# A new order and new engines for every command of a hand-scheduled attention and maxout kernel, later casting loads, no zero products, and a hint for the last jump

## The chip, the core and the metric

The kernel runs on one core of a Trainium2 chip. The metric is device time in microseconds (us): the median of several runs. The core has TensorE (PE in the profile, with its weight loads as PEld), VectorE (DVE), ScalarE (ACT), GpSimd (POOL) and SyncE (SP). A "q" behind a name (SPq, POOLq, ACTq) means that the engine issues a DMA or handles an instruction that its sequencer does alone.

## The reference

`q`, `k` and `v` have 4 batches, 8 heads, 768 positions and 64 numbers per head, in float32. Half the meaning lies in `is_retrieval`: heads 0, 2 and 6 are retrieval heads with a full causal mask, the other five are streaming heads, where a position sees the 4 first positions and the 64 latest ones.

```python
scores = scale * np.matmul(q, k.transpose(0, 1, 3, 2))
causal = rel >= 0
stream_keep = causal & (is_sink | in_win)      # n_sink = 4, window = 64
scores = np.where(mask[None], scores, -1000000000.0)
a = np.exp(scores - max); a = a / (sum(a) + 1e-09)
x = matmul(a, v)                               # to (3072, 512), heads side by side
h = np.maximum(np.maximum(x @ w1, x @ w2), x @ w3)   # 512 -> 768, three times
out = h @ w_out                                # 768 -> 512, float32
```

## The kernel before

The kernel is compiled for the pattern of retrieval heads that it expects (`GUESS`). It computes everything with that pattern, then compares the flags that it was given and checks that all sums of exponentials are in a sane range. Only if one of the two fails does a general, slow block run behind a jump at the end (L780); with these inputs it does not.

Work is done by batch `b`, and in each batch by halves of 384 positions. For each half, attention comes first, and then the products with the four weight matrices, here called the FFN of that half: 18 groups of four products (L387; matrix 0, 1 or 2 times one block of 128 hidden columns), each followed by a copy or a maximum out of PSUM (L395, L397), and 3 output blocks of 128 rows (L412), each copied out (L418) and stored (L419). That makes 21 steps for each of 8 halves, 168 in all. In batch 0 the 18 groups go through matrix 0 first, then 1, then 2.

There is no scheduler. A long list of strings, `PROGRAM`, gives the order in which commands are recorded, and with it the order of each engine's queue: every engine takes its own instructions strictly in that order. A letter at the end of a command picks the engine: `d` VectorE, `a` ScalarE, `p` GpSimd. The commands are:

- `hl half pair n ss`: plain loads of k and q of batch 0, by SyncE (L185). `cast` makes them float16 (L199), `turnp` transposes them on TensorE and copies the result out (L217, L220), `kx0` builds the extra keys (sinks and previous window, L476, L481).
- `s0 half unit pairs`: one unit of scores of batch 0, products on TensorE (L511, L526) and exponentials on ScalarE (L546). `k0` multiplies a mask in (L558).
- `load b quad`: k and q of a later batch, cast on the way by GpSimd's DMA queue (L236). `turn` transposes them on VectorE (L251), `kx` builds extra keys (L488, L493), `s` is a unit of scores (L597, L614), `k` a mask (L627).
- `load_v` loads v by SyncE (L274), `v` and `y` cast it into the two operands that the second product takes (L436, L448, L450).
- `av b half pair`: the product of weights and v (L646), reciprocal and scaling (L651, L653), and with `D` a transpose by SyncE's DMA queue (L659); without it, `x` transposes on TensorE (L669, L672).
- `w i`: a casting load of weight matrix i by GpSimd's queue (L361; `w 3` is the output matrix, L356).
- `f e`: the next step of the FFN; `e` is the engine of its copy.
- `idle n`: n products of a tile of zeros, 128x512, whose result nothing reads (L295).
- `clear`, `cleark`, `strip`: constant fills on VectorE. `flags`: the comparison of the flags. `check`, `verdict`: the check of the sums. `gs`, `gp`: tiny copies that make SyncE or GpSimd wait for a load.

So where a command stands decides both when its own work can begin and what queues behind it. SyncE's DMA issues also wait for an earlier DMA: eight semaphores go round, and a DMA waits for the one eight before it. The staging tiles of the first loads (`pairs2`, two buffers) make `hl 1 2 2` wait for the casts of the pairs loaded by `hl 0 2 2`.

At the end all five engines load the number of mismatches into a register (L779), compare (L780) and, as that number is 0, go to an empty block and jump over the general one to the end.

Of the kernel before, what the change touches and what calls it, by code (L numbers as in the profile page):

```python
# [10 lines left out]
FP32 = mybir.dt.float32  # L11
INT32 = mybir.dt.int32
# [122 lines left out]
def fast(ctx, tc, keep, q, k, v, is_retrieval, n_sink, window, moe_w1, moe_w2, moe_w3, moe_w_out, w_t, woutt, out):  # L135
    nc = tc.nc
    B, H, S, D = q.shape
    DMdl = out.shape[1]
    DF = moe_w1.shape[1]
    P = 128  # L140
# [151 lines left out]
    def idle_work(n):  # L292
        sink = sps.tile([P, 2, 512], FP32, tag="st", name="st")
        for _ in range(n):
            nc.tensor.matmul(sink[:, 0, :], zero[:, 0:P], zero, start=True, stop=True)  # L295
# [650 lines left out]
```

## Time and profile before

| what | value |
|---|---|
| runs | 202.43, 203.18, 203.58 us; median 203.18 |
| the profiled execution | 202.28 us, of which the span from the first to the last instruction is 200.2 |
| PE busy | 180.6 us, 90% of the span |
| DVE, ACT, POOL busy | 152.4, 99.4, 72.3 us |
| first product with weight matrix 0 | 32.23 us into the span |
| last instruction that computes | ends 193.78 us into the span |

The profiled execution is the one whose rows are read below; it is 0.9 us under the median. PE's busy time is an upper bound of its use, since matmuls overlap and their ends are modelled. The program falls into three stretches: a start in which batch 0 is loaded, turned and scored, up to 32 us; a long middle in which TensorE goes from one FFN step to the next with scores and `av` between them; and a tail of some 7 us behind the last product.

### The profile page before, as it was taken

The numbers are of one execution on the slowest core, as the hardware profiler recorded it, in microseconds if no ns is written. First come the engines' busy times: TensorE is split into PE (matmuls) and PEld (weight loads), VectorE is DVE, ScalarE is ACT, GpSimd is POOL, SyncE is SP. The second block draws the span as 40 slices with busy tenths as digits, with TensorE's granted clock in tenths as the row PEclk, the third lists the DMA queues.
The fourth block names the chain that finished last, engine by engine and source line by source line (L and its number), as shares of the span: only waits on it lengthen the run. The fifth ranks groups of instructions, "written<-read, shape, count | busy, mean of one in ns | idle before, by whom it ended". The sixth has DMA issues, their size and how long they took to land.

```text
span 200.2 us, 4763 instructions
## 1 busy us (share of the span) xinstructions
PE 180.6 (90%) x1833; PEld 106.2 (53%) x1833; DVE 152.4 (76%) x357; ACT 99.4 (50%) x170; POOL 72.3 (36%) x111
## 2 busy tenths in 40 slices
PE   0297798999999999999999999999999999999960
PEld 0244365565555644567556645574566467655530
DVE  4897569999797899998479999793667469877800
ACT  2359758723867666174765584537556350000030
POOL 6134724446798215077092049013571030000000
PEclk9999559999999999999999999999999999999996
DMA  5999999999498958996498141014201511340040
GB/s 143 321 166 210 255 203 202 211 142 208 71 212 201 184 102 182 291 230 128 143 233 159 20 144 57 0 24 123 96 0 23 151 65 22 62 157 4 0 160 11
DMA packets 48424, 26.63 MB, mean 133 GB/s; under 512 B 37259, under 2 KB 43915, under 8 KB 48395
## 3 DMA queue, kind: packets, MB, share of 16 engines
q1 hardware_dynamic: 43786, 18.06, 37.0%
q0 software_dynamic: 4192, 7.87, 22.3%
q8 instruction: 16, 0.26, 0.6%
q10 hardware_dynamic: 416, 0.33, 0.5%
q14 instruction: 14, 0.11, 0.2%
HBM read 25.17 MB, written 6.29 MB: 157 GB/s over the span
## 4 chain that ended last, share of the span: by engine, by line
PE 71%; DVE 11%; DMA 8%; issue 3%; ACT 3%; SPq 2%; DVEq 0%; ACTq 0%
PE yy L387 39%; PE yy L412 11%; PE oacc L646 6%; PE st L597 6%; DMA qs<-in_q_dram 6%; PE yst L387 3%; DVE x L653 2%; DMA xT<-x 2%; DVE hT L397 2%; DVE KQ L251 2%; SPq L185 2%; PE st L526 1%; PE tr L217 1%; DVE acc L397 1%; PE yst L412 1%
## 5 line engine op out<-in xcount | busy, mean ns | idle before, releaser
L614 ACT ACTIVATE pt<-st 128x1024 f16<-128x1024 f32 (+2 forms) x51 | 43.5, 907 | 28.0 <-PE st L597 26.4
L627 POOL TENSOR_TENSOR pt<-pt,strip 128x512 f16<-128x512 f16 (+4 forms) x36 | 35.7, 1008 | 55.4 <-ACT pt L614 52.4
L387 PE MATMUL yy<-xT,w2t 128*128 128x384 f16 x180 | 36.0, 326 | 0.4 <-ACT ot L418 0.4
L387 PE MATMUL yy<-xT,w0t 128*128 128x384 f16 x180 | 35.8, 326 | 0.4 <-DMA xT<-x 0.2
L387 PE MATMUL yy<-xT,w1t 128*128 128x384 f16 x180 | 35.2, 326 | 0.2 <-DVE x L653 0.2
L397 DVE TENSOR_TENSOR acc<-yy,acc 128x384 f16<-128x384 f32 x45 | 24.9, 558 | 10.3 <-PE yy L387 4.7
L412 PE MATMUL yy<-woutt,hT 128*128 128x512 f16 (+1 forms) x138 | 31.4, 375 | 0.4 <-DVE hT L397 0.4
L397 DVE TENSOR_TENSOR hT<-yy,acc 128x384 f16<-128x384 f32 x45 | 24.6, 554 | 3.8 <-PE yy L387 1.6
L395 ACT CAST acc<-yy 128x384 f16<-128x384 f32 x26 | 12.4, 486 | 28.1 <-PE yy L387 28.1
L251 DVE STREAM_TRANSPOSE KQ<-kq 128x384 f32<-128x384 f32 x24 | 25.5, 1132 | 0.0
L387 PEld LDWEIGHTS <-w0t 128*128 128x128 f16 x192 | 18.1, 98 | 13.4 <-issue 1.0
L387 PEld LDWEIGHTS <-w1t 128*128 128x128 f16 x192 | 18.1, 98 | 12.9 <-issue 1.1
L387 PEld LDWEIGHTS <-w2t 128*128 128x128 f16 x192 | 17.5, 97 | 12.4 <-issue 1.3
L412 PEld LDWEIGHTS <-hT 128*128 128x128 f16 x150 | 14.0, 98 | 16.1 <-DVE hT L397 1.7
L546 ACT ACTIVATE pt<-st 128x1024 f16<-128x1024 f32 (+4 forms) x28 | 16.2, 636 | 10.1 <-PE st L526 9.8
L646 PEld LDWEIGHTS <-pt 128*128 128x128 f16 x472 | 18.0, 100 | 3.0 <-issue 0.4
L646 PE MATMUL oacc<-va,pt 128*128 128x65 f16 x392 | 19.0, 197 | 0.0
L653 DVE TENSOR_TENSOR x<-oacc,sums 128x384 f16<-128x384 f32 x32 | 17.8, 557 | 1.1
L627 DVE TENSOR_TENSOR pt<-pt,strip 128x256 f16<-128x256 f16 (+4 forms) x33 | 13.9, 437 | 5.6 <-ACT pt L614 5.6
L597 PE MATMUL st<-KQ 32*128 32x128 f16 (+2 forms) x342 | 15.1, 257 | 0.0
L597 PEld LDWEIGHTS <-KQ 32*128 32x128 f16 x342 | 8.8, 92 | 6.8 <-issue 5.6
L646 PE MATMUL oacc<-vx,pt 128*128 128x65 f16 x80 | 12.3, 193 | 0.0
(106 smaller groups left out, 196.3 us busy)
## 6 DMA issues: line engine op xcount, KB each, us to landing
out_dram<-ot SPq DMA_DIRECT2D x23, 256.0 KB, 3.1
vs<-in_v_dram SPq DMA_DIRECT2D x21, 256.0 KB, 7.3
ks<-in_k_dram SPq DMA_DIRECT2D x8, 192.0 KB, 3.2
qs<-in_q_dram SPq DMA_DIRECT2D x7, 192.0 KB, 4.4
kq<-in_k_dram POOLq DMA_DIRECT2D x3, 384.0 KB, 5.3
kq<-in_q_dram POOLq DMA_DIRECT2D x3, 384.0 KB, 7.1
kq<-in_k_dram POOLq DMA_DIRECT2D x3, 288.0 KB, 6.4
kq<-in_q_dram POOLq DMA_DIRECT2D x3, 288.0 KB, 7.4
```

Source lines behind the costliest of these rows:

```text
L185: eng.dma_start(out=st[:, h : h + 2], in_=src[0, 2 * hp + h : 2 * hp + h + 2, half * HALF : (half + 1) * HALF].rearrange("h (p j) d -> p h ...
L251: nc.vector.transpose(out=dst.rearrange("c (p j) -> c j p", j=n)[:, j0:j1], in_=src.rearrange("c (j i) -> c j i", i=R),)
L387: nc.tensor.matmul(yy[:, 0:HALF], w_t[wi][:, ks, ni * P : (ni + 1) * P], xT[b, half, ks].rearrange("p a t -> p (a t)"), start=(ks == 0), s ...
L395: copy_out[0](out=acc[ni], in_=yy[:, 0:HALF])
L397: nc.vector.tensor_tensor(out=acc[ni] if wi == 1 else hT[ni], in0=yy[:, 0:HALF], in1=acc[ni], op=ALU.max)
L412: nc.tensor.matmul(yo[:, 0:n], hT[ns][:, tb * P : (tb + 1) * P], woutt[:, ns, c : c + n], start=(ns == 0), stop=(ns == NNB - 1),)
L546: nc.scalar.activation(out=pts[0, half, hp, u][:, r0:r1, c0:c1], in_=sts[hp][:, r0:r1, c0:c1], func=AF.Exp, scale=sc,)
L597: nc.tensor.matmul(sts["XY"[g // 2]][:, g % 2, c0 : c0 + n * P], KQ[rows, 0, ki * P : (ki + 1) * P] if kind == "p" else kx[b % 2][quad][ro ...
L614: nc.scalar.activation(out=pts[b, s, xy][:, r0:r1, c0:c1], in_=st[:, r0:r1, c0:c1], func=AF.Exp, scale=sc,)
L627: engine.tensor_tensor(out=x, in0=x, in1=m, op=ALU.mult)
L646: nc.tensor.matmul(o[:, i, r, 0 : D + 1], at[b, h, kind, ki, qi], vv[:, 0 : D + 1], start=(n == 0), stop=(n == len(todo) - 1), skip_group_ ...
L653: nc.vector.tensor_tensor(out=x, in0=o[:, :, :, 0:D], in1=rc.unsqueeze(3).to_broadcast([P, HB, 2, D]), op=ALU.mult,)
```

## The change

All commands are put into a new order and many get another engine. The parts that can be named:

- The start: the constant fills of the masks (`strip`) come first; the first three loads of v now stand between `hl 0 2 2` and `hl 1 0 2`; `w 0` and `load 1 0`, the first loads that cast, are issued behind the casts of the pair (1, 1), and GpSimd reaches `w 1` and `w 2` behind the casts of the last pair (1, 3). Before, `load 1 0` was issued ahead of `hl 1 2 2`'s q.
- Six units of the second half's scores stand ahead of the first `f`, where eight stood before. All four `av` of the first half still do.
- `idle 2` and `idle 8` are gone.
- Casts of v (`v`): 22 on POOL, 5 on ACT, 5 on DVE; before 10, 11 and 11. Masks (`k`): 33 on POOL and 36 on DVE; before 36 and 33.
- `av 1 1` now stands behind FFN step 47 to 49 (before: 58); `turn 2 1 0 1` directly behind step 19 and close behind `load 2 1` at step 18.
- `flags` moves from the start to the middle. Its result is kept as an integer, and `guess` (behind step 100) loads it on all five engines as a hint for the last jump. `read` (behind step 155, thirteen steps ahead of the end) loads the mismatch count, which before was loaded where the program ends. The general block is now the one that follows the branch, so that the usual way is the branch taken, to the place that was hinted.
- The last half's outputs: block 1 is copied by VectorE, blocks 0 and 2 by ScalarE. Block 2 is still split in two, but now both parts are copied and also stored by ScalarE; before, VectorE copied the second part, and SyncE stored the first.

```diff
 PROGRAM = (
-    "clear 1, flags, hl 0 1 1 ss, clear 0, cast 0 0 pp, turnp 0 0 dd, cleark 0, hl 0 2 2 ss",
-    "strip 0 14, cast 0 2 aa, cast 0 1 ap, turnp 0 1 d, kx0 0 0 a, s0 0 0 0, hl 1 0 2 ss",
-    "cast 1 0 dd, turnp 0 2 ad, turnp 1 0 da, cleark 1, load_v 0 0 0 4, cast 1 1 ap, idle 2",
-    "kx0 0 1 a, s0 0 0 1, cast 0 3 dd, s0 0 1 0, s0 0 1 1, strip 14 28, kx0 1 0 p, load_v 0 0 4 4",
-    "v 0 0 3 d, hl 1 2 2 ss, v 0 0 2 d, turnp 0 3 aa, cast 1 2 dd, load 1 0, s0 1 1 0, s0 0 1 3",
...
-    "turn 1 1 1 1, f d, v 0 1 3 a, idle 8, f d, f a, f a, s 1 1, load_v 1 0, k0 3 1 1 p, av 0 1 3",
...
-    "f d, check, f d, f d, f a, f a, f a, f d, f d, f d, gs 1, verdict, f a, f a, f d, f a, f a",
+    "clear 0, hl 0 1 1 ss, strip 14 28, strip 0 14, cast 0 0 pp, turnp 0 0 aa, cast 0 1 ap",
+    "turnp 0 1 a, hl 0 2 2 ss, cast 0 2 dp, cast 0 3 ad, load_v 0 0 0 4, cleark 0, s0 0 1 1",
+    "kx0 0 0 a, s0 0 0 0, kx0 0 1 p, turnp 0 2 ad, kx0 0 2 p, turnp 0 3 da, hl 1 0 2 ss",
+    "cast 1 0 da, cast 1 1 pp, load_v 0 0 4 4, s0 0 1 2, y 0 0 4:5:1 s d, cleark 1, w 0",
+    "v 0 0 2 a, turnp 1 0 aa, v 0 0 1 p, turnp 1 1 d, s0 0 1 0, load 1 0, kx0 0 3 p, v 0 0 3 p",
+    "hl 1 2 2 ss, cast 1 2 da, s0 0 0 1, y 0 0 5:8:2 r p, y 0 0 4:5:1 r a, clear 1, v 0 0 0 d",
...
+    "check, f d, f d, f d, verdict, f d, f a, f a, f a, f a, f d, read, f d, f d, f a, f a, f a",
+    "f d, f d, f d, f a, f a, f a, f a, f a",
 )
...
-            for c, op, eng in (
-                (0, nc.scalar.copy if last else copy_out[0], nc.sync),
-                (n, nc.vector.tensor_copy, nc.scalar),
-            )[:parts]:
+            for c in range(0, DMdl, n):
...
+                op = copy_out[0] if not last else nc.vector.tensor_copy if tb == 1 else nc.scalar.copy
                 op(out=ot[:, c : c + n], in_=yo[:, 0:n])
-                eng.dma_start(out=out[r0 : r0 + P, c : c + n], in_=ot[:, c : c + n])
+                (nc.sync if parts == 1 else nc.scalar).dma_start(
+                    out=out[r0 : r0 + P, c : c + n], in_=ot[:, c : c + n]
+                )
...
+        nc.vector.tensor_copy(out=flagged, in_=other.to_broadcast([1, 2]))
...
+    def read():
+        found["n"] = nc.values_load(differ[0:1, 0:1], min_val=0, max_val=1 << 20)
+
+    def guess():
+        likely = nc.values_load(flagged[0:1, 0:1], min_val=0, max_val=H)
+        E = mybir.EngineType
+        tc.mark_branch_hint_location("last", likely, [E.SP, E.PE, E.Activation, E.DVE, E.Pool])
...
-        n = nc.values_load(differ[0:1, 0:1], min_val=0, max_val=1 << 20)
-        with tc.If(n > 0, preferred_fallthrough_block=False):
+        with tc.If(n > 0, preferred_fallthrough_block=True, label="last"):
```

More of the change, by code (lines that the diff above doesn't have):

```diff
@@ L292, in idle_work @@
     def idle_work(n):
-        sink = sps.tile([P, 2, 512], FP32, tag="st", name="st")
+        sink = bank([P, 512], FP32, "idl")
         for _ in range(n):
-            nc.tensor.matmul(sink[:, 0, :], zero[:, 0:P], zero, start=True, stop=True)
+            nc.tensor.matmul(sink, zero[:, 0:P], zero, start=True, stop=True)
     warm = consts.tile([P, 2], FP32, name="warm")
@@ L674, in fast @@
     differ = keep.tile([1, 2], INT32, name="differ")
+    flagged = keep.tile([1, 2], INT32, name="flagged")
     found = {}
@@ L744, in fast @@
         w=lambda wi, *p: load_weight(int(wi), *map(int, p)),
+        read=read,
+        guess=guess,
     )
@@ L749, in fast @@
             do[name](*args)
-    return differ
+    return found["n"]
 def kernel(
@@ L774 @@
         xs_dram = tc.dram_tile([B * H, S, D], FP16, name="xs_dram")
-        differ = fast(
+        n = fast(
             tc, keep, q, k, v, is_retrieval, int(n_sink), int(window),
```

90 rows, old and new, of the table PROGRAM are left out of this document.

## The prediction

> **What bounds the kernel now.** I read the page's first part, the busy time by stretch, the chain of waits, and then the groups and DMA issues that the change touches. First the busy time of the engines in six stretches that I cut at the first product with weight matrix 0 (32.23 us) and at the end of the last product (columns: stretch, its length, PE, PEld, DVE, ACT, POOL, granted clock, DMA share, GB/s):
>
> ```profile
> 0.00:4.65 4.65, 0.00 (x0) 0.00 (x1) 2.29 (x10) 1.49 (x2) 3.01 (x13) 1.00 0.50 140
> 4.65:32.23 27.58, 20.91 (x183) 11.73 (x184) 20.93 (x79) 17.75 (x40) 11.94 (x24) 0.81 1.07 228
> 32.23:60.00 27.77, 27.66 (x308) 16.16 (x305) 26.03 (x51) 16.44 (x30) 16.47 (x21) 1.00 0.97 172
> 60.00:100.00 40.00, 39.17 (x444) 22.98 (x443) 33.51 (x70) 24.20 (x38) 16.54 (x22) 1.00 0.83 182
> 100.00:193.36 93.36, 92.85 (x906) 55.27 (x903) 69.20 (x149) 39.47 (x64) 24.30 (x33) 1.00 0.29 75
> 193.36:200.20 6.84, 0.00 (x0) 0.00 (x0) 0.42 (x1) 0.00 (x0) 0.00 (x0) 0.74 0.26 86
> ```
>
> From 32.23 to 193.36 TensorE is busy 27.66 + 39.17 + 92.85 = 159.68 of 161.13 us. So the middle is bound by TensorE, and only 1.45 us of its idle time can be won there. VectorE, with 26.03 of 27.77 us in the third stretch, is the next bound. The start has 4.65 + 6.67 = 11.3 us without a product, and the tail 6.8 us. That is where an order can win; in the middle it can mostly lose. The chain of waits tells what the start waits for:
>
> ```profile
> 3.71 4.42 DMA qs<-in_q_dram
> ...
> 13.65 0.52 ACT kn L199
> ...
> 15.18 6.92 DMA qs<-in_q_dram
> ...
> 22.23 0.55 DVE qn L199
> ...
> 32.68 1.95 PE yy L387 x11
> 34.62 0.43 PE st L526 x7
> ...
> 36.46 0.48 PE st L526 x3
> ...
> 44.86 1.73 PE st L295 x8
> ...
> 193.36 0.42 DVE ot L418
> ```
>
> A late cast (13.65) frees the staging tile for the last pairs of k and q; their q is issued at 15.18 and takes 6.92 us, where an early one takes 4.42. All that follows up to the first product leans on it.
>
> **The start.** SyncE's queue, and then GpSimd's, show what stood ahead of that load and what ran beside it:
>
> ```profile
> 5.81 0.98 SPq L185 DMA_DIRECT2D qs<-in_q_dram  x2
> ...
> 6.87 4.55 SPq L274 DMA_DIRECT2D vs<-in_v_dram  x6
> ```
> ```profile
> 14.07 0.73 POOL L236 DMA_DIRECT2D kq<-in_k_dram  x1 [0.23 <-issue]
> ...
> 20.36 0.82 POOL L361 DMA_DIRECT2D w0t<-in_moe_w_dram  x1
> ...
> 22.46 0.75 POOL L361 DMA_DIRECT2D w1t<-in_moe_w_dram  x1
> 23.20 0.75 POOL L361 DMA_DIRECT2D w2t<-in_moe_w_dram  x1
> ```
> ```profile
> w0t<-in_moe_w_dram POOLq DMA_DIRECT2D x1, 768.0 KB, 9.5
> w1t<-in_moe_w_dram POOLq DMA_DIRECT2D x1, 768.0 KB, 12.0
> w2t<-in_moe_w_dram POOLq DMA_DIRECT2D x1, 768.0 KB, 15.4
> ```
>
> The casting load of 14.07 goes through the same DMA engines (share 1.07). The new order casts the pairs of the first half before everything else, and puts no casting load ahead of the first half's plain loads. So SyncE can issue that q load when the DMA eight places before it has landed. That one is a q load of the pairs before, issued at 5.81 here; with three v loads ahead of it (4.55 / 6 = 0.76 us each) it goes out at 8.1 and, with the early load's 4.42, lands at 12.5. The last q load then lands near 12.5 + 4.4 = 16.9 instead of 22.1: 5.2 us sooner. Not all of it arrives at TensorE. Between 22.2 and 32.2 the chain holds 10 us of casts, copies, exponentials and small products; ScalarE works 17.75 and TensorE 20.91 of the 27.58 us, so they soon become what the start waits for. The bounds are 0 and 5.2 us; I take two thirds, 3.5, as the engines are well filled but 6.67 us without a product lie in the stretch. The first product then stands at 28.7.
>
> The weights cover this. `w 0` waits only for casts that I place at 13 to 14 us, some 6 us sooner than 20.36, so 9.5 us later it lands by 24. `w 1` and `w 2` stand behind the casts of the last pair, at some 20 us: landed by 32 and by 35.4, with 12.0 and 15.4. They are wanted after six and after twelve groups of 0.65 us (1.95 us for eleven products is three groups) with two score units before each, at 28.7 + 4.8 = 33.5 and at 38.3. If the start gained more than 5.0 us, `w 1` would be what is late next.
>
> Two units of scores that stood ahead of the first FFN step now stand behind it, where TensorE is full: 0.43 + 0.48 = 0.9 us back.
>
> `idle 2`, in the start, is counted there. `idle 8` is 1.73 us in a full TensorE, and I take 1.7. Its bounds are 0 and 1.73: if VectorE were late there anyway, the gap stays as a wait.
>
> One rule is weighed here. The rows around the half clock, and at `idle 8`:
>
> ```profile
> 18.00:20.00 2.00, 1.33 (x14) 0.87 (x13) 0.52 (x2) 1.87 (x6) 0.91 (x3) 0.78 1.07 254
> 20.00:24.00 4.00, 3.99 (x31) 1.77 (x29) 1.73 (x4) 3.15 (x8) 3.82 (x7) 0.50 1.21 269
> 24.00:28.00 4.00, 2.93 (x18) 1.39 (x18) 2.96 (x9) 2.10 (x4) 0.00 (x0) 0.50 1.15 202
> 28.00:30.00 2.00, 2.00 (x35) 1.77 (x35) 1.12 (x5) 1.17 (x4) 1.06 (x3) 0.66 1.15 200
> 30.00:32.00 2.00, 1.60 (x26) 1.00 (x28) 1.93 (x6) 1.95 (x4) 2.00 (x5) 1.00 1.16 202
> 44.00:47.00 3.00, 3.00 (x18) 1.57 (x17) 3.00 (x5) 1.82 (x3) 1.50 (x1) 1.00 1.25 190
> ```
>
> The granted clock is 0.50 from 20 to 28 us, though TensorE counts as busy for 3.99 of the first 4 us, and full from 30 us on, with and without zeros. The Trainium skill ("TensorE: Matmul & The Clock Gate", The HAM clock gate) says that about 3.4 us of sustained products release the full clock and that an idle window takes it away; by it, dropping zeros speaks against the change in the gappy start and costs nothing at 44 us. This trace does not bear the first part out: 3.99 busy us released nothing. By the skill's rule a denser start would run at full clock; rival (e) prices that from rows.
>
> **The middle.** The work is the same and only its places change. From the lists: 12 more casts of v and 3 masks fewer on GpSimd, 6 casts fewer each on VectorE and ScalarE, and 3 masks more on VectorE. The prices:
>
> ```profile
> L627 POOL TENSOR_TENSOR pt<-pt,strip 128x512 f16<-128x512 f16 x19 | 22.0, 1163 | 31.2 <-ACT pt L614 31.1
> L436 DVE CAST va<-vs 128x384 f16<-128x384 f32 x11 | 5.7, 524 | 0.0
> L436 POOL CAST va<-vs 128x384 f16<-128x384 f32 x10 | 5.1, 524 | 0.0
> L627 DVE TENSOR_TENSOR pt<-pt,strip 128x512 f16<-128x512 f16 x11 | 5.5, 498 | 2.9 <-ACT pt L614 2.9
> ```
> ```profile
> POOL pt L627 <- ACT pt L614: 52.4, 11, 11.2
> PEld L387 <- issue: 3.3, 12, 0.7
> ```
>
> GpSimd gets 12 x 0.524 - 3 x 1.163 = +2.8 us, VectorE 3 x 0.498 - 6 x 0.524 = -1.7. Both lie beside TensorE's work, with VectorE's share somewhat eased. What can show is a queue: a cast behind a mask whose exponentials come late. The gain is bounded by the 1.45 us of idle time, the loss by one such wait of 11.2 us. An order this dense, started earlier, meets VectorE at its fullest, so I take a loss of 1.0. The two register loads per engine (`guess`, `read`) make TensorE's sequencer stop twice. The nearest row is its waits called issue, up to 0.7 us, so 0 to 1.4; I take 0, as weights loaded ahead cover them, and without that cover they cost the 1.4.
>
> **The tail.** SyncE's waits and the last store:
>
> ```profile
> SPq L780 <- SPq L780: 1.7, 1, 1.7
> ```
> ```profile
> out_dram<-ot ACTq DMA_DIRECT2D x1, 128.0 KB, 3.1
> ```
> ```profile
> 192.75 0.37 ACT L418 COPY ot<-yst 128x256 f32<-128x256 f32 x1
> 193.82 0.37 ACTq L419 DMA_DIRECT2D out_dram<-ot  x1
> ```
>
> The last store lands at 193.82 + 3.1 = 196.9, and the span ends 3.3 us later. SyncE waits 1.7 us at the jump for nobody but itself. The hint can win from 0 to 3.3; I take 1.6, the wait that the row shows, less a little. The Trainium skill ("Runtime: NRT & Kernel Launch", Instruction fetch mechanics) says that a taken branch out of the fetched window stalls for its code. The self-wait agrees; by the skill's rule alone the tail would gain 0. What a hint does to the wait, no row here shows.
>
> ScalarE now copies and stores both parts of the last block: free of the first part at 193.12, it issues to 193.49, copies to 193.86 and issues then, 0.04 behind 193.82. I put 0.1.
>
> **The sum.** -3.5 + 0.9 - 1.7 + 1.0 - 1.6 + 0.1 = -4.8 us against the profiled execution's 202.28 (span 200.2 and 2.08 around it): 197.5. The median shown, 203.18, is 0.9 higher; against it the sum gives 198.4, which is my forecast.
>
> **The rivals.**
>
> (a) The start stays: ScalarE or a TensorE at half clock binds it, whatever lands sooner. For it: 20.91 of 27.58 us busy at a mean clock of 0.81. Against it: the 6.67 us without a product there. Time: 198.4 + 3.5 = 201.9 at most; with half of the gain kept 200.1. I call it 201.
>
> (b) The hint does nothing, and the taken jump waits as before: 198.4 + 1.6 = 200.0.
>
> (c) VectorE takes the start's gain back, being busy 26.03 of 27.77 us already; each us that TensorE comes sooner is then met by a wait on VectorE: 3.5 and 0.9 lost, 202.8. Against it: it loses 1.7 us of casts.
>
> (d) Slower: GpSimd's queue. 22 casts of v stand there among masks that wait for exponentials. In the FFN steps 35 to 47 I count 6 of these casts, 4 masks, 2 k/q issues and more, some 10 us, against some 13 us of TensorE, right ahead of `av 1 1`, which needs all of them. If one wait of 11.2 us falls there, the cover is 3 us, and 8 us show: 206. It decides from 5.8 us on (4.8, and 1.0 for half a percent). Against it: GpSimd is idle for nearly two thirds of the span.
>
> (e) The half clock of 20 to 28 us goes: its 6.92 busy us halve, 3.5 us if TensorE binds there: 194.9.
>
> **How the numbers follow.** The forecast 0.40, (a) 0.18, (b) 0.10, (c) 0.10, (d) 0.16, (e) 0.06. Half a percent, 1.0 us, is about what a measurement of this kernel can tell from no change, so same is 202.2 to 204.2. Faster: 0.40 + 0.18 + 0.10 + 0.06, which is 0.74. Same: (c), 0.10. Slower: (d), 0.16. The range is 194.0 to 204.5: its lower end is (e) with a better middle, its upper end leaves out (d) and no more. The forecast's own range is 196 to 200.5.
>
> **What would show it.** Right: the first product with matrix 0 near 28.7 us; the q load that took 6.92 us landed before 18; no zero products; PE idle 1 to 4 us from there to the last product; that last product to the span's end in some 5.3 us, with the wait of 1.7 at the jump gone. Wrong: a first product behind 31 us, waits of TensorE on GpSimd's masks or VectorE's `hT` in batch 0 or 1 of over 2 us in all, weights 1 or 2 waited for, or a tail still near 6.8 us.

## The result

The changed kernel takes 200.98 us (median of 9 runs, 198.93 to 204.06), the kernel before 202.97 us (median of 9, 202.41 to 203.58). The ratio is 0.985, with an interval of 0.982 to 0.988: about 1.5% faster, where 198.4 us was forecast; the medians alone give 1.0%. The changed kernel's executions scatter over 5 us, those of the kernels made from it over 3 to 10, where before's scatter over 1.2. The ratios take the executions within 1.5% of the same kernel's fastest, so medians and extremes stand beside them below.

The profiled execution took 200.64 us, its span 198.9. Busy time by stretch, cut at the first product with weight matrix 0 (now at 25.76 us) and at the end of the last product (193.95), with the columns of before:

```profile
4.65:25.76 21.11, 17.46 (x173) 10.45 (x173) 17.19 (x62) 16.36 (x39) 9.93 (x23) 1.00 1.13 250
25.76:60.00 34.24, 31.46 (x333) 17.43 (x331) 27.27 (x48) 22.79 (x38) 19.52 (x29) 0.95 1.03 176
60.00:100.00 40.00, 37.49 (x457) 22.09 (x459) 34.59 (x74) 24.09 (x35) 21.65 (x32) 1.00 0.86 166
100.00:193.95 93.95, 92.71 (x878) 54.63 (x869) 73.46 (x153) 33.94 (x55) 22.67 (x33) 1.00 0.31 80
193.95:198.90 4.95, 0.01 (x1) 0.00 (x0) 0.00 (x0) 0.37 (x1) 0.00 (x0) 0.81 0.33 113
```

| part | forecast | before | after | difference |
|---|---|---|---|---|
| start, to the first product with matrix 0 | -3.5 | 32.23 | 25.76 | -6.5 |
| from there to the end of the last product | +0.2 (0.9 - 1.7 + 1.0) | 161.1 | 168.2 | +7.1 |
| tail | -1.5 (-1.6 + 0.1) | 6.9 | 4.9 | -2.0 |
| span | -4.8 | 200.2 | 198.9 | -1.3 |

So the start gave nearly twice what was forecast, the tail a little more, and the middle took all of the start's gain back. In the middle TensorE is busy 31.46 + 37.49 + 92.71 = 161.7 of 168.2 us: 6.5 us idle, where before it was 1.45. Nearly all of that lies before 105 us. Of the +7.1 us, 5.1 are this idle time and 2.0 are busy time, the half clock named below among it. TensorE's waits there (engine, line, what for, us in total, times, longest), and the stretch around the first of them:

```profile
PE yy L388 <- DMA w1t<-in_moe_w_dram: 2.0, 1, 2.0
PE yy L388 <- DMA xT<-x: 1.8, 3, 0.9
PE st L598 <- ACT pt L615: 1.0, 2, 0.6
...
PE yy L388 <- DVE ot L417: 0.5, 1, 0.5
PE yy L388 <- DVE x L654: 0.5, 1, 0.5
```
```profile
30.16:32.53 2.37, 0.33 (x4) 0.01 (x1) 0.71 (x3) 0.51 (x2) 1.96 (x5) 1.00 1.16 202
32.53:37.00 4.47, 4.47 (x19) 2.16 (x21) 1.80 (x4) 0.00 (x0) 0.00 (x0) 0.62 1.15 208
```

TensorE first waits for weight matrix 1, and right behind that wait the granted clock is 0.50 for 3.41 us (33.18 to 36.60), which costs half of it, some 1.7 us. The next waits are for the transposing DMAs of batch 1 (`xT`, to 76.6 us), for exponentials that stand behind the copy of a late load of v on ScalarE (85 to 87 us), and behind VectorE at 100 to 104 us. The chain shows what held VectorE there, and GpSimd's timeline what ran beside it:

```profile
96.00 0.54 DVE none L687
96.56 2.05 DVE both L689
98.63 1.08 DVE both L690
```
```profile
95.34 4.98 POOL L628 TENSOR_TENSOR pt<-pt,strip 128x512 f16<-128x512 f16 x4
```

These are the operations of `flags` on 8 or 16 numbers. In the start of the kernel before, each took some 0.15 us; in the middle, beside four masks on GpSimd, the two with two inputs took 2.05 and 1.08, and the first one, with one input, 0.54.

### The profile page after: what moved, and what is told of

Same layout as the page of the kernel before. It is cut to its first block, busy times and chain, and to the rows that moved or that the text cites. A ratio compares the mean times of both kernels' runs of the same rounds, so it can differ in the third digit from the quotient of the medians.

```text
span 198.9 us, 4761 instructions
## 1 busy us (share of the span) xinstructions
PE 179.2 (90%) x1823; PEld 104.6 (53%) x1823; DVE 154.8 (78%) x345; ACT 99.0 (50%) x167; POOL 76.8 (39%) x127
## 4 chain that ended last, share of the span: by engine, by line
PE 48%; DVE 5%; ACT 1%; issue 1%; ACTq 0%; DVEq 0%
PE yy L388 29%; PE yy L410 8%; PE oacc L647 4%; PE st L598 3%; PE yst L388 3%; DVE KQ L252 1%; DVE both L689 1%; PE yst L410 1%; DVE hT L398 1%; DVE both L690 1%; ACT pt L615 0%; ACT ot L417 0%; DVE acc L398 0%; DVE x L654 0%; DVE none L687 0%
## 5 line engine op out<-in xcount | busy, mean ns | idle before, releaser
L628 POOL TENSOR_TENSOR pt<-pt,strip 128x512 f16<-128x512 f16 (+5 forms) x33 | 32.5, 1003 | 42.5 <-ACT pt L615 39.5
L388 PE MATMUL yy<-xT,w1t 128*128 128x384 f16 x180 | 37.1, 339 | 2.0 <-DMA w1t<-in_moe_w_dram 2.0
L388 PEld LDWEIGHTS <-w1t 128*128 128x128 f16 x192 | 18.6, 101 | 17.0 <-issue 3.3
L396 ACT CAST acc<-yy 128x384 f16<-128x384 f32 x27 | 12.9, 481 | 24.6 <-PE yy L388 21.2
L628 DVE TENSOR_TENSOR pt<-pt,strip 128x512 f16<-128x512 f16 (+5 forms) x36 | 19.0, 541 | 1.2 <-ACT pt L615 1.2
L647 PEld LDWEIGHTS <-pt 128*128 128x128 f16 x472 | 17.4, 97 | 3.6 <-issue 0.7
L647 PE MATMUL oacc<-va,pt 128*128 128x65 f16 x392 | 19.1, 194 | 0.1
L437 POOL CAST va<-vs 128x384 f16<-128x384 f32 x22 | 11.7, 541 | 6.8 <-DMA vs<-in_v_dram 6.7
```

Source lines behind the costliest of these rows:

```text
L388: nc.tensor.matmul(yy[:, 0:HALF], w_t[wi][:, ks, ni * P : (ni + 1) * P], xT[b, half, ks].rearrange("p a t -> p (a t)"), start=(ks == 0), s ...
L396: copy_out[0](out=acc[ni], in_=yy[:, 0:HALF])
L437: op(out=va[b % 2][:, hs, half * HB : (half + 1) * HB, 0:D], in_=staged_v[b, half][:, hs],)
L628: engine.tensor_tensor(out=x, in0=x, in1=m, op=ALU.mult)
L647: nc.tensor.matmul(o[:, i, r, 0 : D + 1], at[b, h, kind, ki, qi], vv[:, 0 : D + 1], start=(n == 0), stop=(n == len(todo) - 1), skip_group_ ...
```

## The experiments

Times are medians with the extremes, ratios are to the kernel before, with a 95% interval in brackets.

**`flags` back in the start.**

```diff
-    "turnp 0 1 a, hl 0 2 2 ss, cast 0 2 dp, cast 0 3 ad, load_v 0 0 0 4, cleark 0, s0 0 1 1",
+    "turnp 0 1 a, hl 0 2 2 ss, cast 0 2 dp, cast 0 3 ad, load_v 0 0 0 4, flags, cleark 0, s0 0 1 1",
...
-    "f d, f d, k 2 0 X 0 p, f a, s 2 5, v 2 0 0 p, k 2 5 Y 0 p, f a, flags, k 2 1 X 1 d, f d",
+    "f d, f d, k 2 0 X 0 p, f a, s 2 5, v 2 0 0 p, k 2 5 Y 0 p, f a, k 2 1 X 1 d, f d",
```

> The changed kernel with the comparison of the flags back in the start (ahead of `cleark 0`), nothing else moved. Theory (lock): the small VectorE operations that took 0.58, 2.04 and 1.07 us beside GpSimd's masks at 95.3 to 100.3 us take some 0.15 us each again, the 4 us of VectorE come back, and TensorE's waits of 0.66 and 0.67 us at 100.6 and 103.1 us go: 1.3 us less than the changed kernel, ratio to before near 0.979. Rival (VectorE is late there anyway): the waits stay or move on by a step, and the time changes by less than 0.4 us (ratio 0.983 to 0.987).

Measured: 205.04 us (199.66 to 210.13), ratio 0.988 [0.982, 0.994]. The lock itself is as the theory had it; two rows of VectorE's timeline in the start:

```profile
9.52 0.16 DVE L687 TENSOR_SCALAR none<-ir 1x16 f32<-1x16 int32 x1
...
9.72 0.15 DVE L689 TENSOR_TENSOR both<-none 1x8 f32<-1x8 f32 x1
```

Between 100 and 105 us TensorE no longer waits. But the kernel is not faster (its median is 4 us above the changed one's), and this profile (span 204.0) shows another wait in its place:

```profile
76.13 0.58 POOL L237 DMA_DIRECT2D kq<-in_k_dram  x1
...
81.90 0.48 PE L388 MATMUL yy<-xT,w0t 128*128 128x384 f16 x1 [4.38 <-DMA xT<-x]
```

The fourth transposing DMA of batch 1 took 5.9 us to land, where it took 2.3 in the changed kernel's profile. TensorE waited 2.3 us for an earlier one of the four, up to 75.9 us, and 4.4 us for this one, and the granted clock is 0.50 from 76.2 to 86.4 us. What differs is taken up below.

**v of the second half behind weight matrix 0.** The gate (`gs 0`) makes SyncE wait for matrix 0, which landed at 23.96 us in the changed kernel.

```diff
-    "y 0 0 1:4:2 s d, load_v 0 1, s0 0 0 2, kx0 1 0 a, turnp 1 2 dd, s0 0 0 3, s0 0 1 3",
+    "y 0 0 1:4:2 s d, gs 0, load_v 0 1, s0 0 0 2, kx0 1 0 a, turnp 1 2 dd, s0 0 0 3, s0 0 1 3",
...
-    "k0 0 0 0 p, f a, f a, f d, kx 1 0 p, turn 1 1 0 1, w 3, s0 1 1 3, f d, gs 0, s0 1 3 3",
+    "k0 0 0 0 p, f a, f a, f d, kx 1 0 p, turn 1 1 0 1, w 3, s0 1 1 3, f d, s0 1 3 3",
```

> The changed kernel with the plain v loads of the second half held behind the gate on weight matrix 0, so that they no longer share the DMA engines with weights 0 and 1. Theory (weight 1 is late, and its wait costs the clock): weight 1, landed at 32.48 us before, lands by 30.2; TensorE's wait of 2.0 us goes and the 3.4 us at half clock behind it too (1.7 us of products): 3.7 us less than the changed kernel, ratio to before near 0.967, and the runs scatter by 1 to 2 us in place of 5. First rival (the half clock has another cause): the wait goes, the half clock stays, 2.0 us less (ratio 0.975). Second rival (the DMA engines were not what weight 1 waited for): it lands within 0.5 us of 32.5 and the time stays (0.983 to 0.987).

Measured: 199.79 us (197.21 to 202.92), ratio 0.978 [0.973, 0.984]. Matrix 1 landed 11.0 us after its issue in place of 12.6, the wait is short, and the clock stays full behind it (timeline, and a row by stretch):

```profile
30.81 2.45 PE L388 MATMUL yy<-xT,w1t 128*128 128x384 f16 x14 [0.58 <-DMA w1t<-in_moe_w_dram]
```
```profile
32.00:36.00 4.00, 4.00 (x30) 2.09 (x28) 3.75 (x9) 1.51 (x2) 0.47 (x2) 1.00 1.13 211
```

So the transfers were what matrix 1 waited for, and the wait was what cost the clock. Of the 3.7 us expected, 3.3 are won there, and little of that arrives: compared at the same FFN step, this kernel is 3.3 us ahead of the changed one near 38 us, 1.6 past the wait for `xT` and 0.9 at 135. By the ratio it gains 0.7%, with intervals that overlap, so a gain in time is not shown; the scatter stays.

**No hint.**

```diff
-    "s 3 2, k 3 2 X 1 d, av 2 1 0 D, k 3 2 Y 0 d, av 2 1 2 D, av 2 1 3 D, f a, guess, f a, s 3 1",
+    "s 3 2, k 3 2 X 1 d, av 2 1 0 D, k 3 2 Y 0 d, av 2 1 2 D, av 2 1 3 D, f a, f a, s 3 1",
```

> The changed kernel without the hint (its register loads and the hint itself left out; the order of the two blocks behind the jump as in the changed kernel). Theory (the hint fetches the code behind the jump): from the end of the last product to the span's end 6 to 7 us in place of 4.9, with a jump on TensorE or SyncE that takes 2 to 4 us again; 1 to 2 us slower than the changed kernel. Rival (the order of the blocks alone removes the stall): tail 4.9 us as in the changed kernel, time the same.

Measured: 203.76 us (199.12 to 206.94, four executions), too scattered for a verdict; the tail is read from the trace, with times from the end of the last product:

| | before | changed | no hint |
|---|---|---|---|
| TensorE's jump: begins, takes | +0.19, 3.69 | -2.75, 0.40 | -2.75, 3.65 |
| SyncE's jump begins | +2.47, behind the wait for its own last store (landed at +1.95) | -0.17 | -0.12 |
| SyncE's next instruction | +5.22 | +2.74 | +2.80 |
| last store of all, issued by ScalarE, has landed | +3.64 | +2.77 | +4.43 |
| SyncE stops for that one | no | no | 0.8 |
| span ends | +6.9 | +4.9 | +5.8 |

The hint takes TensorE's jump from 3.65 to 0.40 us, but TensorE is through its jump by +0.9 us without it too, long before the end. Behind SyncE's jump 2.8 us pass with and without the hint, 0.3 us more than the landing that its next instruction waits for (+2.4). The 0.9 us of the tail are another wait, in SyncE's list without the hint:

```profile
SPq L954 <- DMA out_dram<-ot: 0.8, 1, 0.8
```

The last store took 3.84 us to land where it took 2.17 in the changed kernel: 15 of its 16 parts had landed by +2.8, the last one at +4.43. Among the DMA packets of this trace is a transfer of 16 KB of instructions from +1.6 to +3.2 us, where the changed kernel has none. The same holds for all profiles here: in the three without a hint (this one, before, before without zeros) such a transfer runs beside the last store, and the store takes 3.1 to 3.8 us; in the eleven with a hint there is none, and it takes 2.2 to 2.5. So the hint most likely wins by keeping a fetch of code off the last store; that the one holds up the other is argued, not shown. The tails with a hint go from 4.9 to 5.6 us, so one profile of 5.8 is no exact price either.

The other 1.1 us are won without the hint too: SyncE jumps ahead of its wait for the stores, not behind it, and so the 2.8 us behind its jump and the landings pass at the same time. The Trainium skill ("Runtime: NRT & Kernel Launch", Instruction fetch mechanics) has a taken branch out of the fetched window stall; TensorE's 3.65 us agrees, and it says nothing of a hint.

**Zeros in the wait for matrix 1.**

```diff
-    "k0 1 0 1 p, s0 1 2 0, k0 2 0 2 d, f a, f d, k0 0 1 1 p, k0 1 1 1 d, f a, f d, load 1 1",
+    "k0 1 0 1 p, s0 1 2 0, k0 2 0 2 d, f a, f d, k0 0 1 1 p, k0 1 1 1 d, f a, idle 10, f d, load 1 1",
```

> The changed kernel with ten products of zeros (ten of 0.22 us at full clock) ahead of the first FFN step with weight matrix 1, where TensorE waits 2.0 us. Theory (the wait takes the clock away): weight 1 still lands near 32.5 us, the granted clock stays 1.00 from 20 us on, and the products behind the wait stand 0.16 apart in place of 0.32: 1.7 us less than the changed kernel (ratio to before near 0.977). Rival (the half clock at 33 to 37 us has another cause, or comes later by as much): the stretch at 0.50 stays, and the time is the same or up to 0.2 us more (0.985 to 0.986).

Measured: 201.47 us (199.77 to 203.88), ratio 0.990 [0.985, 0.995]. The theory is right on the clock and wrong on the time:

```profile
30.68 2.32 PE L296 MATMUL idl<-zero 128*128 128x512 f16 x10
```
```profile
33.00:37.00 4.00, 4.00 (x30) 2.30 (x29) 3.06 (x6) 1.04 (x2) 0.00 (x0) 1.00 1.16 210
```

At the same FFN step it is 1.4 us ahead of the changed kernel at 40 us and 0.2 at 100. What is won ahead of 73 us is lost at the waits that follow, as in the run with the gate.

**Batch 2's loads behind batch 1's transposing DMAs.** Both v loads of batch 2, half 0 first, and the casts that need them; and the casting load of batch 3 (`load 3 0`) behind these casts.

```diff
-    "load_v 2 1, f a, k 1 0 X 0 d, v 1 0 0 d, f d, f d, s 1 6, k 1 3 Y 0 d, y 1 0 1:8:2 r p, f d",
-    "f a, av 1 0 1 D, v 1 1 1 p, f a, av 1 0 0 D, s 1 4, v 1 0 3 p, av 1 0 2 D, v 2 1 0 p, f a",
-    "k 1 4 Y 0 p, av 1 0 3 D, y 1 1 4:5:1 r d, f a, v 1 1 2 p, load_v 2 0, f a, k 1 7 Y 1 d",
-    "v 2 1 3 p, turn 2 0 0 0, k 1 7 X 0 d, f a, load 3 0, k 1 7 Y 0 p, turn 2 0 1 1, f a",
+    "f a, k 1 0 X 0 d, v 1 0 0 d, f d, f d, s 1 6, k 1 3 Y 0 d, y 1 0 1:8:2 r p, f d",
+    "f a, av 1 0 1 D, v 1 1 1 p, f a, av 1 0 0 D, s 1 4, v 1 0 3 p, av 1 0 2 D, f a",
+    "k 1 4 Y 0 p, av 1 0 3 D, load_v 2 0, y 1 1 4:5:1 r d, f a, v 1 1 2 p, load_v 2 1, f a, k 1 7 Y 1 d",
+    "turn 2 0 0 0, k 1 7 X 0 d, f a, k 1 7 Y 0 p, turn 2 0 1 1, f a",
...
-    "k 1 4 X 1 p, k 1 6 X 0 p, v 1 1 0 p, kx 2 0 p, av 1 1 1 D, f a, av 1 1 0 D, v 2 1 2 p",
+    "k 1 4 X 1 p, k 1 6 X 0 p, v 1 1 0 p, kx 2 0 p, av 1 1 1 D, f a, av 1 1 0 D, v 2 1 0 p, v 2 1 3 p, v 2 1 2 p, load 3 0",
```

> The changed kernel with batch 2's v loads and batch 3's first k/q load put behind the four transposing DMAs of batch 1 (v of half 0 first), and the casts that wait for them with them. Theory (transfers asked for too early crowd the transposing DMAs): the four issues of 2.23, 1.74, 1.21 and 1.21 us from 68.8 us take some 1.2 each, TensorE's waits on `xT` (1.8 us in the changed kernel's profile, 7.3 in the one with the flags early) fall below 0.7, ScalarE's wait of 2.25 us for v at 84.4 us goes with v of half 0 asked for first, and the slow executions of 202 to 210 us go: median 198 to 199.5, ratio 0.970 to 0.980, scatter below 3 us. Rival (the DMA engines are full up to 90 us whatever the order): the waits move to v or k/q of batch 2, time 200 to 202 (0.983 to 0.995) and the scatter stays.

Measured: 203.66 us (202.68 to 207.01), ratio 1.004 [1.002, 1.006]. The waits on `xT` are gone from the profile, but `load 3 0` went out 10 us too late, and VectorE, which turns it, held TensorE at 88 us:

```profile
85.91 0.58 POOL L237 DMA_DIRECT2D kq<-in_k_dram  x1
...
91.88 1.13 DVE L252 STREAM_TRANSPOSE KQ<-kq 128x384 f32<-128x384 f32 x1 [6.29 <-DMA kq<-in_k_dram]
```

The edit mixed two things and is repeated below with the load earlier.

**No stores of batch 0.**

```diff
+                if b > 0:
...
```

> The changed kernel without the stores of batch 0's result (1.5 MB out of the traffic between 50 and 88 us; the copies into the staging tile stay; batch 0 of the output is not written). Theory (up to 90 us the middle is bound by what the DMA engines have brought): some 7 us of DMA time at 210 GB/s go, the waits on `xT`, v and the exponentials at 73 to 87 us shrink by 1 us or more, 1 to 3 us less than the changed kernel (ratio 0.970 to 0.980), scatter down. Rival (each wait is a fault of its own place in the order): the same waits stand, time within 0.5 us of the changed kernel (0.983 to 0.987).

Measured: 199.63 us (195.25 to 203.01), ratio 0.966 [0.962, 0.970]. The ratio rests on two of seven executions (195.25 and 196.47); the medians give 0.985, against 0.990 for the changed kernel. The fastest execution is 3.7 us below the changed kernel's fastest. That speaks for the theory, but it does not show that the DMA engines are full: the edit also takes six issues off SyncE's queue, and up to 73 us this profile stays within 0.4 us of the changed kernel's at the same FFN step. The scatter did not go down, and the profile (span 201.3) shows the wait of the first experiment again: casting load and fourth transposing DMA were issued at the same time.

```profile
73.67 0.58 POOL L237 DMA_DIRECT2D kq<-in_k_dram  x1
...
79.67 0.32 PE L388 MATMUL yy<-xT,w0t 128*128 128x384 f16 x1 [4.30 <-DMA xT<-x]
```

**A casting load at the head of GpSimd's queue.**

```diff
-    "clear 0, hl 0 1 1 ss, strip 14 28, strip 0 14, cast 0 0 pp, turnp 0 0 aa, cast 0 1 ap",
+    "clear 0, hl 0 1 1 ss, strip 14 28, strip 0 14, load 1 0, cast 0 0 pp, turnp 0 0 aa, cast 0 1 ap",
...
-    "v 0 0 2 a, turnp 1 0 aa, v 0 0 1 p, turnp 1 1 d, s0 0 1 0, load 1 0, kx0 0 3 p, v 0 0 3 p",
+    "v 0 0 2 a, turnp 1 0 aa, v 0 0 1 p, turnp 1 1 d, s0 0 1 0, kx0 0 3 p, v 0 0 3 p",
```

> The changed kernel with the casting loads of batch 1's first k and q put at the head of GpSimd's queue, ahead of the first casts (in the changed kernel at 15.5 us, behind all plain loads of the first half). Theory (the start was won by keeping casting loads out of the first half's plain loads): the last q load lands at 20 us or later in place of 17.6, the first product with weight matrix 0 starts at 28 us or later in place of 25.8, and the time is 1.5 us or more above the changed kernel's. Rival (the start was won by the order of the casts and by the engines alone): first product within 0.7 us of 25.8, and the time the same or less, as k and q of batch 1 land sooner.

Measured: 202.88 us (199.48 to 205.22), ratio 0.991 [0.987, 0.995]. The last q load landed at 21.3 us in place of 17.6, and the first product came at 29.80 in place of 25.76 us. The theory held for the start: the place of the casting loads moves it one to one. How much of that reaches the time is less clear (1.2 us by the ratios, 1.9 by the medians, 1.5 or more expected). The trace shows how it melts: at the same FFN step this kernel is 4.0 us behind the changed one at 30 us, 0.2 at 40 and 1.3 at 68. Matrix 1, landed at 33.36 us, is not waited for, and the clock stays full there. So of 4.0 us of start less than a third is left 40 us later; the larger losses of this profile lie at `xT`, behind 73 us.

**The kernel before without its zeros.**

```diff
-    "cast 1 0 dd, turnp 0 2 ad, turnp 1 0 da, cleark 1, load_v 0 0 0 4, cast 1 1 ap, idle 2",
+    "cast 1 0 dd, turnp 0 2 ad, turnp 1 0 da, cleark 1, load_v 0 0 0 4, cast 1 1 ap",
...
-    "turn 1 1 1 1, f d, v 0 1 3 a, idle 8, f d, f a, f a, s 1 1, load_v 1 0, k0 3 1 1 p, av 0 1 3",
+    "turn 1 1 1 1, f d, v 0 1 3 a, f d, f a, f a, s 1 1, load_v 1 0, k0 3 1 1 p, av 0 1 3",
```

> The kernel before without its products of zeros (two in the start, eight at 44.9 us, 1.73 us). Theory (the eight cost their full time): 1.5 to 1.7 us less than before, ratio 0.992, TensorE idle no longer than before there. Rival (they filled a wait, or kept the clock): a wait or a stretch at half clock stands in their place, time the same (0.998 to 1.002) or more.

Measured: 208.06 us (207.51 to 208.10), ratio 1.027 [1.024, 1.029]: 5.4 us slower. Both rivals in one, and more. TensorE's waits, and the stretches behind the second:

```profile
48.33 0.40 PE L597 MATMUL st<-KQ 32*128 32x256 f16 x5 [1.38 <-DVE KQ L251]
60.52 3.75 PE L387 MATMUL yy<-xT,w0t 128*128 128x384 f16 x13 [3.81 <-DMA xT<-x]
```
```profile
56.00:60.00 4.00, 0.71 (x4) 0.29 (x3) 1.55 (x3) 1.13 (x2) 3.86 (x6) 1.00 1.15 168
60.00:64.00 4.00, 3.48 (x13) 1.73 (x13) 1.92 (x4) 0.18 (x1) 3.79 (x6) 0.57 1.30 238
```

The eight zeros (1.73 us) stood in a wait for VectorE's transposition, which is there without them (1.38 us). And the shift turned the order of two DMAs: before, the transposing DMA goes out at 52.15 us and the casting load of GpSimd at 52.88; here the casting load goes at 52.85 and the transposing DMA at 53.66. That one lands after 6.8 us in place of 4.0, TensorE waits 3.8 us, and the clock is halved for 3.41 us.

Laid side by side, the profiles show how narrow this is (us; the fourth transposing DMA of batch 1, in the two upper rows the one of batch 0):

| kernel | transposing DMA issued | casting load issued later by | transposing DMA lands after |
|---|---|---|---|
| before | 52.15 | 0.73 | 4.0 |
| before without zeros | 53.66 | -0.81 | 6.8 |
| flags early | 75.96 | 0.17 | 5.9 |
| no stores of batch 0 | 73.67 | 0.00 | 6.0 |
| zeros in the wait | 73.79 | 1.06 | 2.3 |
| changed | 74.26 | 1.24 | 2.3 |
| casting load later | 74.35 | 3.59 | 2.3 |

The Trainium skill ("DMA: Bandwidth & Descriptors", Issuing engines are not separate DMA queues) says that DMAs of all engines run on the same 16 DMA engines and interleave. The table agrees, and adds a price: in the rows of batch 1, between 0.17 and 1.06 us in the issue lie 3.6 us in the landing.

**The casting load of batch 3 later.**

```diff
-    "v 2 1 3 p, turn 2 0 0 0, k 1 7 X 0 d, f a, load 3 0, k 1 7 Y 0 p, turn 2 0 1 1, f a",
-    "turn 2 0 0 1, f d, turn 2 0 1 0, f d, f a, f a, v 1 1 3 p, k 1 4 X 0 d, k 1 6 Y 0 p, s 2 0",
+    "v 2 1 3 p, turn 2 0 0 0, k 1 7 X 0 d, f a, k 1 7 Y 0 p, turn 2 0 1 1, f a",
+    "turn 2 0 0 1, f d, turn 2 0 1 0, f d, f a, f a, v 1 1 3 p, load 3 0, k 1 4 X 0 d, k 1 6 Y 0 p, s 2 0",
```

> The changed kernel with the casting load of batch 3's first k and q moved on GpSimd's queue behind one mask and one cast of v (some 1.7 us of work), nothing else. In the profiles so far that load was issued 1.24 us (changed kernel), 1.18 and 1.40 us after the fourth transposing DMA of batch 1 where that landed in 2.3 us, and 0.00 and 0.17 us after it where it took 5.96 and 5.90 us, TensorE waited 4.3 to 4.4 us and then ran 3.4 to 10 us at half clock. Theory (this race is what makes the executions differ by 5 us): with the load 2.9 us behind, every execution has the short landing; runs above 202 us go, median 199.5 to 200.5 and scatter below 2.5 us. Rival (the scatter has other causes): some executions still take over 202 us, scatter 4 us or more, median near 201.

Measured: 200.61 us (198.18 to 202.72), ratio 0.980 [0.974, 0.986]. One execution still took over 202 us and the scatter is 4.5 us, so the rival stands: the race alone is not what makes the executions differ. Nor is the clock alone: the executions of 198.18 and 202.72 us had mean granted clocks of 0.998 and 0.997.

**Four edits at once**: this later load, `flags` early, the gate, and

```diff
-    "load_v 3 1, y 2 0 1:8:2 s a, av 1 1 3 D, s 2 1, k 2 0 Y 0 d, f a, v 2 1 1 p, k 2 1 X 0 p",
+    "load_v 3 1, y 2 0 1:8:2 s p, av 1 1 3 D, s 2 1, k 2 0 Y 0 d, f a, v 2 1 1 p, k 2 1 X 0 p",
```

> The changed kernel with four edits: that casting load later, the comparison of the flags back in the start, the second half's v behind the gate on weight matrix 0, and the copy of batch 2's first v rows moved from ScalarE, where exponentials stood behind it, to GpSimd. Theory (each of the waits costs its own time once the race is gone, as nothing else binds TensorE behind them): the waits for weight 1 (2.0), at the flags (1.3) and at 85 to 87 us (1.4) and 1.7 us of half clock go: 195 to 197 us, ratio 0.960 to 0.970, scatter below 3 us. Rival (what is won ahead of 73 us is met by transfers that come no sooner): 198 to 200 us, ratio 0.975 to 0.985, with longer waits on `xT`, v or k/q of batches 1 and 2.

Measured: 201.04 us (196.83 to 202.13), with one execution below 200. The rival's account held, at a time 1 us above its range. The first FFN step of batch 1 takes `xT` in four parts, one from each transposing DMA. Rows of its product on the last part, in the changed kernel, the one with the later load, and this one:

```profile
76.61 0.32 PE L388 MATMUL yy<-xT,w0t 128*128 128x384 f16 x1 [0.95 <-DMA xT<-x]
```
```profile
76.72 0.32 PE L388 MATMUL yy<-xT,w0t 128*128 128x384 f16 x1 [0.72 <-DMA xT<-x]
```
```profile
77.82 0.32 PE L388 MATMUL yy<-xT,w0t 128*128 128x384 f16 x1 [0.95 <-DMA xT<-x]
```

At 68 us the later load was 0.6 us ahead of the changed kernel and this one 0.9; behind the wait they are 0.1 and 1.2 us late. The gate alone, 2.6 us ahead at 68 us, comes to this product at 75.05 and keeps 1.6. So a lead shrinks at this wait, but TensorE does not come back at one time in all kernels, although the next expectation says so.

**The transposing DMAs first, again**, as above, with `load 3 0` near 76 us (78.8 in the profile).

```diff
-    "k 1 4 X 1 p, k 1 6 X 0 p, v 1 1 0 p, kx 2 0 p, av 1 1 1 D, f a, av 1 1 0 D, v 2 1 2 p",
+    "k 1 4 X 1 p, k 1 6 X 0 p, load 3 0, v 1 1 0 p, kx 2 0 p, av 1 1 1 D, f a, av 1 1 0 D, v 2 1 0 p, v 2 1 3 p, v 2 1 2 p",
```

> The changed kernel with both v loads of batch 2 and the casting load of batch 3 behind the transposing DMAs of batch 1, as in the run with the loads behind them, but the casting load 10 us sooner than there (near 76 us; there it went out at 85.9 us, landed at 94, and VectorE's transposition of it held TensorE for 5.4 us). Theory (in all profiles TensorE comes back at 75.4 us, whatever was won ahead, because the four transposing DMAs stand behind v and k/q that were asked for at 61 to 64 us): the first lands by 72 us in place of 73.7 to 74.6, the wait there falls below 0.7 us, no wait of 5 us stands at 88 us, and the time is 198 to 199.5 us (ratio 0.972 to 0.982). Rival (batch 2's v, later by 10 us, is waited for in its turn): 200 to 203 us, with a wait of 1 us or more at 84 to 95 us on v, KQ or a mask behind a cast.

Measured: 203.48 us (201.99 to 206.70), ratio 1.001 [0.999, 1.004]. The time is the rival's or a little over, but its cause is another one. At `xT` the edit works, though the first transposing DMA landed at 74.1 us: this kernel is 1.7 us behind the changed one at 68 us and 2.6 ahead at 99. Then comes one wait of 4.6 us, not for batch 2's v but on a mask of GpSimd that stands behind a copy of batch 3's v:

```profile
98.76 0.60 POOL L449 CAST vx<-vs 64x512 f16<-64x512 f32 x1 [4.54 <-DMA vs<-in_v_dram]
99.44 4.97 POOL L628 TENSOR_TENSOR pt<-pt,strip 128x512 f16<-128x512 f16 x4
```

**The same with the gate and `flags` at a quiet place of GpSimd.**

```diff
-    "y 3 0 4:5:1 s a, f a, k 2 6 Y 0 d, s 3 0, f a, y 3 0 1:8:2 r a, f d, f d, av 2 1 1 D, f d",
+    "y 3 0 4:5:1 s a, f a, flags, k 2 6 Y 0 d, s 3 0, f a, y 3 0 1:8:2 r a, f d, f d, av 2 1 1 D, f d",
```

> The kernel of the run before with two more edits: the second half's v behind the gate on weight matrix 0, and the comparison of the flags put where GpSimd has little to do (near 130 us). Theory (with the transposing DMAs free, what is won ahead of 73 us is kept): first wait for weight 1 below 0.8 us and no half clock, the lead of 3 us at 38 us still there at 100 us, the two waits behind the flags gone: 195 to 197 us (ratio 0.960 to 0.970). Rival (the next transfer takes the lead back): the lead is below 1.5 us at 100 us, time 198 us or more.

Measured: 200.96 us (199.61 to 202.83), ratio 0.988 [0.986, 0.991]. The lead holds past 73 us, and then the next transfer takes it:

```profile
95.42 4.96 POOL L628 TENSOR_TENSOR pt<-pt,strip 128x512 f16<-128x512 f16 x4
```
```profile
100.44 0.40 PE L647 MATMUL oacc<-va,pt 128*128 128x65 f16 x4 [4.73 <-POOL pt L628]
```
```profile
98.00:106.00 8.00, 5.56 (x25) 2.91 (x26) 2.02 (x5) 0.99 (x2) 7.88 (x13) 0.57 0.10 27
```

At the same FFN step this kernel was 7.2 us ahead of the changed one at 99.6 us of the latter, and 0.9 us behind at 105. Batch 3's v landed at 94.6 us; the copy and four masks behind it on GpSimd run from there to 100.4, at the same time as in the changed kernel (95.34 to 100.3). This v was not held up on its way: SyncE issued it at 89.9 to 91.1 us, behind two transposing DMAs (85.43 and 87.27), and it landed 3.5 to 4.6 us later, as fast as the early loads. It was asked for late. None of the kernels that store the whole result is shown to beat the changed one; the gate alone comes nearest, with 199.79 us.

## Why the prediction was right, and where it was not

The sign was right and the time 2.6 us too low, above the forecast's own range (196 to 200.5). That it came so close is luck in part: the start and the tail gave 3.5 us more than the sum had, and the middle lost 6.9 us more. Point by point:

- **The start** was mis-sized: -3.5 forecast, -6.5 measured, beyond the bound of -5.2. The load came as worked out: the q load forecast for 16.9 us landed at 16.97 (issued 0.6 us later than forecast, and 0.5 faster), and the last one at 17.6, 5.2 us sooner than before. That only two thirds would arrive failed: all of it arrived, and 1.3 us more, since the step from the last q to the first product shrank from 9.4 to 8.1 us at a clock that is full from 19.5 us on. That fits the mechanism of rival (e), at a third of its price; no run separates it. Rival (a) fell. The experiment with the casting load first shows that the load order did it: 3.7 us on the load, 4.0 on the first product.
- **What is late next** was named and then left out of the sum: "if the start gained more than 5.0 us, `w 1` would be what is late next". It gained 6.5, matrix 1 landed at 32.48 us (forecast 32), and TensorE waited 2.0 us for it, with 1.7 us of half clock behind. The prediction itself had named this wait as a sign of being wrong.
- **`idle 8` at -1.7** was wrong for its place: its lower bound, "if VectorE were late there anyway, the gap stays as a wait", is what the kernel before showed without it (a wait of 1.38 us), and the shift of two DMAs that came with it cost 5.4 us in all. What leaving the zeros out is worth in the new order, no run prices.
- **The middle at +1.0** is the step that failed: +7.1 measured, against +0.2 with the scores and the zeros. Its limit was taken from the profile of before, in which TensorE was the bound, and it was so in part because its start was late. Summed from the GB/s by stretches of 10 us, by 60 us the DMA engines had moved some 11.7 MB before and 11.9 after, by 100 us 19.0 and 18.6. TensorE came 6.5 us sooner to data that came no sooner. The casting load put first shows it from the other side (4.0 us lost in the start, 1.3 left at 68 us), and the edits that won 1.4 to 3.5 us by 40 us lost most of it at `xT` or at 100 us. That is rival (c) with another engine: late data takes the start's gain back, not VectorE. Why the data is late stays open in part. In the changed kernel the loads of v, k and q issued at 62.6 to 63.8 us take 7 to 10 us to land, which fits full DMA engines; in the last experiment batch 3's v is issued late on SyncE's queue and lands fast. No run separates the two for the whole stretch.
- **Rival (d)**, a cast of v on GpSimd with masks behind it, is not what the changed kernel met at `av 1 1`. It stands at the v copy of batch 3, and became the largest wait of the middle (4.7 us) as soon as TensorE reached it early.
- **The tail** was forecast at 1.6 and gave 2.0, by luck: the row it rests on was misread. The 1.7 us that SyncE "waits at the jump for nobody but itself" is its wait for its own last store, issued at 193.15 us and landed at 195.27. So that row is no stall of a jump. The jump is the 2.7 us behind it, and it is not shown to be gone: 2.8 us pass there in the changed kernel, beside the landings. Of the 2.0 us, 1.1 come with the order of the blocks, which was not priced, and 0.9 with the hint, through the last store. Rival (b) fell in its price; for SyncE's jump it may be right.
- **The register loads** (0.49 and 0.31 us on TensorE, at 132.4 and 181.0 us) show as no wait between products: taken at 0, as forecast.

Left open: why the executions of one kernel differ by 5 us. Two profiles show one cause, the late transposing DMA with a half clock around it; the kernel with that race moved apart scatters nearly as much, with two executions of the same mean clock 4.5 us apart.

## What to carry to other kernels

A busy TensorE in the profile of a tuned kernel says what binds it at that pace. Before a gain at the start is added to the sum, the landings of the later loads should be compared with the times at which the work would reach them; here they would have told that the middle could keep little. Where data is late, look first whether it was asked for late or came slowly. A wait of 2 us can also cost the clock behind it, and two DMAs of different engines that are issued within a microsecond of each other are a race that any edit upstream can turn.

## What was unexpected of the hardware

- From 20 us to the last product, stretches at half clock last a multiple of 3.41 us (3.41, 6.83 and 10.24 were seen). The length of a wait alone does not decide: 2.04 us for matrix 1 halved the clock in the changed kernel, 2.14, 2.21 and 2.25 us for it did not in three others (batch 2's loads behind batch 1's transposing DMAs, the later casting load, `flags` early). Where the wait lies decides: cut each of the fourteen profiles into stretches of 3.41 us, counted from a change of the clock. In all twelve at full clock that a half clock follows, TensorE is idle for 1.94 us or more by the busy times of the profile, in all others at full clock for 1.81 or less; the three waits that cost nothing are each cut in two by such an edge. In the start it does not hold: 1.41 us idle came before the halving at 19.1 us in the kernel before. Ten products of zeros in the wait kept the clock full. The Trainium skill ("TensorE: Matmul & The Clock Gate", What's actually happening) has a free-running window of 3413 ns; the multiples agree. Its rule (the same page, HAM oscillation — how this bites in real kernels) that there be no idle gaps over some 3.4 us is too generous: 2.04 us cost the clock.
- A VectorE operation on 8 numbers took 2.05 us beside GpSimd's masks, and 0.15 us away from them. The Trainium skill ("SBUF — State Buffer", SBUF: two separate sides) says that a VectorE operation with two SBUF inputs and a GpSimd operation that reads SBUF exclude each other for a whole instruction; the rows of the two operations with two inputs agree. The one with one input, 0.54 us there, is not covered by it.
- A hint 58 us ahead of the jump took it from 3.65 to 0.40 us on TensorE; the 2.8 us behind SyncE's jump stayed.
